# Lending dead SBUF as exp output buffers in a two-layer transformer kernel

## The chip, the cores and the metric

The kernel runs on one core of one Trainium2 chip. The metric is device time in microseconds (us) of one execution. The kernel before ran at a median of 1637.42 us in three runs.

## The reference, cut to what matters

Two identical layers are applied to a sequence of 2048 positions of width 512. Each is attention with 32 heads of 16 columns, then a feed-forward block with 1792 hidden columns. Both layers use the same weights.

```python
# inside _A_ref, which sees the layer-normed x
scores = jnp.einsum("bhqd,bhkd->bhqk", q, k) * (Dh ** -0.5)
p = _softmax(scores, axis=-1)
o = jnp.einsum("bhqk,bhkd->bhqd", p, v)
# the whole network
x = x + _A_ref(_layernorm(x, axis=-1), A_wqkv, A_wo)
x = x + _B_ref(_layernorm(x, axis=-1), B_w1, B_b1, B_w2, B_b2)
x = x + _A_ref(_layernorm(x, axis=-1), A_wqkv, A_wo)
x = x + _B_ref(_layernorm(x, axis=-1), B_w1, B_b1, B_w2, B_b2)
```

## The kernel before

The work is cut into 4096 score tiles of 128 keys by 512 query columns. For each tile TensorE (PE) makes the scores in PSUM, some engine makes the exponentials, and PE multiplies them with V (the "PV matmuls"). ScalarE (ACT) makes most exponentials with its own exp, two or three tiles in one instruction, into a ring of 15 SBUF units of 128x512 called PT. VectorE (DVE) makes the others by integer arithmetic on the bits, into other buffers; such a tile costs PE four PV matmuls in place of one. A unit of PT is free again when its PV matmul has read it.

The Python file is a planner: it runs a list scheduler with a cost model, and writes one fixed instruction order for each engine with semaphore waits. So a change of buffers changes the order of everything behind it. The PV matmuls go pass by pass (a pass is one group of heads for one segment of queries) through one PSUM bank. A pass must end, and VectorE must copy or add its result, before the PV matmuls of the next pass can begin.

The parts that matter, with cuts marked `# ...`:

```python
PT_RING = 15
PTLOW = 5
PTURG = 6
# ...
    def units(self, n):            # n free units at equal distances
        free = sorted(self.s.pools["pt"])
        # ...
    def exps(self):
        # ...
            if self.units(n) is None:              # no buffer: ScalarE waits
                self.starved = n
                yield ("cond", lambda n=n: self.units(n) is not None)
        # ...
            dst = T["PT"][:, run[0]:run[-1] + 1:step, :]
            yield _Op("act", 0.065 + 0.4267 * n, lambda e, src=src, dst=dst: e.activation(
                out=dst, in_=src, func=ACT.Exp, scale=0.25), # ...
    def pvs(self):
        # ...
            def urge():            # priority of the PV matmuls; small goes first
                return 0.5 if len(pools["pt"]) < PTURG or len(pools["du"]) < DUURG else PVP
        # ... whose tile is read first, ScalarE's (aq) or VectorE's (dq)
                        order = [self.aq[k], self.dq[k]]
                        if len(pools["pt"]) > PTLOW:
                            order.reverse()
```

Two marks count free units: with fewer than 6 free the PV matmuls become urgent, and with more than 5 free PE reads VectorE's tiles before ScalarE's. Where PE would idle, the planner puts filler matmuls that are meant to keep its clock up (with more of them the mean granted clock was 0.989 in e9 against 0.985, and in e10 0.987 against 0.987 in the same call); the constant `WARM` (0.38) says how busy it wants PE to be.

The softmax here doesn't subtract the row's maximum and nothing guards it: scores larger than these inputs give would overflow.

## Time and profile before

| | kernel before |
|---|---|
| span of the profiled run | 1631.0 us |
| ScalarE busy / idle | 1565.6 / 65.5 us |
| tiles on ScalarE / VectorE | 3254 / 842 |
| ScalarE waits on PV matmuls (no free unit) | 17.4 us |
| ScalarE waits for scores | 10.7 us |

The first line of the page (busy time of each engine, share of the span, instructions), and the first line of the chain that ended last:

```profile
PE 1443.1 (88%) x13642; PEld 417.7 (26%) x13794; DVE 1336.9 (82%) x2579; ACT 1565.6 (96%) x1413; POOL 111.9 (7%) x143
...
ACT 70%; PE 26%; DVE 2%; issue 1%; DMA 0%; POOL 0%
```

The groups with shapes kept apart. The columns are line, engine, operation, output<-input, shapes, count, then busy us and mean ns of one, then the idle time of the engine before them and what ended it:

```profile
L1313 ACT ACTIVATE pt<-ps 128x1024 bf16<-128x1024 f32 x815 | 848.6, 1100 | 15.1 <-PE ps L1374 9.3 <-PE ps L1059 4.9
L1313 ACT ACTIVATE pt<-ps 128x1536 bf16<-128x1536 f32 x541 | 821.8, 1519 | 15.9 <-PE ps L1374 8.0 <-PE ps L1059 5.7
...
L1204 DVE TENSOR_SCALAR du<-ps 128x512 uint16<-128x512 f32 x631 | 427.2, 685 | 132.9 <-PE ps L1059 126.5
...
L1204 DVE TENSOR_SCALAR dh<-ps 128x512 uint16<-128x512 f32 x113 | 77.5, 686 | 19.7 <-PE ps L1059 18.6
...
L1204 DVE TENSOR_SCALAR kt<-ps 128x512 uint16<-128x512 f32 x98 | 67.2, 686 | 22.2 <-PE ps L1059 21.3
```

The waits of ScalarE (who waited for whom: us in total, times, longest us):

```profile
ACT pt L1313 <- PE ps L1374: 17.4, 12, 3.5
ACT kt L645 <- PE ps L635: 14.9, 2, 13.7
ACT pt L1313 <- PE ps L1059: 10.7, 27, 1.4
```

ScalarE is the bound: it is busy for 96% of the span. L1313 is the exp, L1374 the PV matmul, L1059 the score matmul, L1204 the first step of VectorE's exp; its three counts add up to 842 tiles. Only the first line of the waits is about exp buffers; the second is the start, where the first projection is awaited. The exp line is busy 1487.1 us for 3254 tiles (the page's group of both shapes), 0.457 us per tile on average.

### The profile page before, as it was taken

The page shows a single profiled execution, that of the slowest core. Times are in us where ns is not written, and L with a number is a line of the kernel's source. Part 1 is how long each engine was busy: PE and PEld are TensorE (multiplying, and loading weights), DVE is VectorE, ACT ScalarE, POOL GpSimd, SP SyncE. Part 2 cuts the span into 40 slices and gives each one's busy share as a digit, 9 for nine tenths or more (in the row PEclk, how much of TensorE's full clock was granted, in tenths as well). Part 3 has the DMA queues.
Part 4 walks back from the last instruction along what each step waited for, and adds up shares of the span by engine and source line. Part 5 has one row for each costly group of instructions (what it writes and reads, how often), then busy time and mean ns, then how long its engine had stood idle before and what let it go on. Part 6 is the DMA issues. An engine that isn't in the chain of part 4 may idle for free.

```text
span 1631.0 us, 32568 instructions
## 1 busy us (share of the span) xinstructions
PE 1443.1 (88%) x13642; PEld 417.7 (26%) x13794; DVE 1336.9 (82%) x2579; ACT 1565.6 (96%) x1413; POOL 111.9 (7%) x143
## 2 busy tenths in 40 slices
PE   6998888898988989899898998888989889889997
PEld 2222222222222222222222222222222222233334
DVE  6579889778887797887888878998988997898883
ACT  5999999999999999999999999988999999999995
POOL 3200000000000000000100001010000000000000
PEclk9999999999999999999999999998999999999999
DMA  5100001100111001110111001001101100011121
GB/s 172 23 1 1 1 14 27 33 1 20 42 31 33 1 21 40 34 33 1 24 42 33 27 1 27 27 2 33 40 8 33 33 14 11 5 34 40 31 63 39
DMA packets 88317, 44.82 MB, mean 27 GB/s; under 512 B 33645, under 2 KB 88174, under 8 KB 88174
## 3 DMA queue, kind: packets, MB, share of 16 engines
q1 hardware_dynamic: 88174, 42.75, 9.8%
q8 instruction: 110, 1.80, 0.5%
q14 instruction: 33, 0.27, 0.1%
HBM read 33.03 MB, written 2.10 MB: 22 GB/s over the span
## 4 chain that ended last, share of the span: by engine, by line
ACT 70%; PE 26%; DVE 2%; issue 1%; DMA 0%; POOL 0%
ACT pt L1313 66%; PE ps L1374 8%; PE ps L1059 8%; ACT g L850 3%; PE ps L635 3%; PE ps L817 2%; PE ps L863 2%; PE ps L632 1%; PE ps L744 1%; ACT L850 1%; PE ps L1046 1%; ACT L1313 1%; DVE du L1204 0%; DVE du L1267 0%; DMA x<-in_A_x_dram 0%
## 5 line engine op out<-in xcount | busy, mean ns | idle before, releaser
L1313 ACT ACTIVATE pt<-ps 128x1536 bf16<-128x1536 f32 (+1 forms) x1357 | 1487.1, 1267 | 31.0 <-PE ps L1374 17.4
L1059 PE MATMUL ps<-qp,kt 32*128 32x512 bf16 x4096 | 550.3, 387 | 140.0 <-ACT pt L1313 111.1
L1204 DVE TENSOR_SCALAR du<-ps 128x512 uint16<-128x512 f32 x631 | 427.2, 685 | 132.9 <-PE ps L1059 126.5
L1374 PE MATMUL ps<-pt,v 128*17 128x512 bf16 (+1 forms) x3656 | 450.5, 361 | 2.9 <-DVE kt L707 0.8
L1374 PE MATMUL ps<-du,vc 128*17 128x512 bf16 (+1 forms) x2115 | 328.8, 360 | 0.8 <-DVE du L1267 0.7
L1059 PEld LDWEIGHTS ps<-qp,kt 32*128 32x128 bf16 x4096 | 143.8, 91 | 697.2 <-ACT pt L1313 334.6
L1267 DVE TENSOR_SCALAR du<-du 128x2048 uint16<-128x2048 uint16 (+1 forms) x319 | 218.2, 688 | 2.8
L1374 PE MATMUL ps<-du,v 128*17 128x512 bf16 (+1 forms) x705 | 170.6, 360 | 0.8 <-DVE kt L1267 0.5
L1023 POOL TENSOR_SCALAR qp<-q,mask 128x512 bf16<-128x512 bf16 (+1 forms) x92 | 68.6, 745 | 1285.2 <-PE ps L1059 1276.0
L1374 PEld LDWEIGHTS ps<-pt,v 128*17 128x17 bf16 x3656 | 103.8, 88 | 149.7 <-issue 118.2
L1265 DVE TENSOR_SCALAR du<-du 128x1024 uint16<-128x1024 uint16 (+1 forms) x319 | 129.9, 414 | 3.3
L863 PE MATMUL ps<-w,g 128*128 128x512 bf16 x396 | 115.7, 385 | 10.7 <-issue 5.4
L817 PE MATMUL ps<-xf,wr 128*128 128x512 bf16 (+1 forms) x420 | 113.4, 362 | 8.0 <-issue 5.6
L1374 PE MATMUL ps<-dh,vc 128*17 128x512 bf16 (+1 forms) x375 | 110.2, 365 | 0.0
L1374 PEld LDWEIGHTS ps<-du,vc 128*17 128x17 bf16 x2115 | 87.5, 90 | 62.1 <-issue 33.8
L1204 DVE TENSOR_SCALAR dh<-ps 128x512 uint16<-128x512 f32 x113 | 77.5, 686 | 19.7 <-PE ps L1059 18.6
L831 DVE TENSOR_SCALAR g<-ps,hb1t 128x512 bf16<-128x512 f32 (+1 forms) x112 | 79.7, 712 | 16.1 <-PE ps L817 15.3
L1204 DVE TENSOR_SCALAR kt<-ps 128x512 uint16<-128x512 f32 x98 | 67.2, 686 | 22.2 <-PE ps L1059 21.3
L1046 PE MATMUL ps<-w 128*32 128x512 bf16 x713 | 70.2, 397 | 0.1
L1374 PE MATMUL ps<-kt,vc 128*17 128x512 bf16 (+1 forms) x366 | 67.1, 340 | 0.0
L1374 PEld LDWEIGHTS ps<-du,v 128*17 128x17 bf16 x705 | 43.8, 89 | 27.7 <-issue 16.4
L1267 DVE TENSOR_SCALAR dh<-dh 128x1024 uint16<-128x1024 uint16 x113 | 47.7, 422 | 1.0
(74 smaller groups left out, 959.9 us busy)
## 6 DMA issues: line engine op xcount, KB each, us to landing
wr<-in_B_w_dram SPq DMA_DIRECT2D x59, 256.0 KB, 2.9
wr<-in_A_wqkv_dram SPq DMA_DIRECT2D x24, 256.0 KB, 2.8
wr<-in_A_wo_dram SPq DMA_DIRECT2D x18, 256.0 KB, 2.8
x<-in_A_x_dram SPq DMA_DIRECT2D x4, 512.0 KB, 8.4
out_dram<-x SPq DMA_DIRECT2D x16, 128.0 KB, 1.7
w<-in_B_w_dram SPq DMA_DIRECT2D x1, 1792.0 KB, 11.1
g<-in_A_wqkv_dram SPq DMA_DIRECT2D x3, 512.0 KB, 6.2
kt<-in_B_w_dram SPq DMA_DIRECT2D x4, 256.0 KB, 3.2
```

The lines of the kernel that those rows point to most:

```text
L817: fns = [lambda e, dc=dc, j=j, pb=pb: e.matmul(pb, lhsT=T["WR"][w][:, 256 * dc + 128 * j:256 * dc + 128 * j + 128], rhs=T["XF"][:, dc, q], ...
L831: yield _Op("dve", 0.21 + n / 966, lambda e, fc=fc, pb=pb: e.tensor_scalar(T["G"][:, fc, q], pb, T["HB1T"][:, fc:fc + 1], None, op0=ALU.ad ...
L850: fns.append(lambda e, g=g: e.activation(out=g, in_=g, func=ACT.Gelu_apprx_tanh))
L863: fns = [lambda e, fc=fc: e.matmul(pb, lhsT=T["G"][:, fc, q], rhs=T["W2"][:, fc, :], start=(fc == 0), stop=False) for fc in range(NFC)]
L1023: yield _Op("pool", 0.1 + 0.6 * w / 512, lambda e, s=s, q=q, i=i, t=t, w=w: e.tensor_scalar(T["QP"][:, s, w * i:w * i + w], q, T["MASK"][: ...
L1046: fns.append(lambda e, o=o, a=a, m=m: e.matmul(o, lhsT=T["W2"][:, 0, m * a:m * a + m], rhs=T["W2"][:, 1, :], start=True, stop=True, tile_p ...
L1059: return (lambda e: e.matmul(o, lhsT=lhsT, rhs=rhs, start=True, stop=True, tile_position=(32 * a, 0)), ["K%d.%d.%d" % (l, gb, kt // 4), "Q ...
L1204: yield _Op("dve", 0.68, lambda e: e.tensor_scalar(u, self.bank(b), E_SCALE, E_BIAS, op0=ALU.mult, op1=ALU.add), reads=["B.%d" % b], write ...
L1265: yield _Op("dve", 0.08 + 0.14 * n, lambda e: e.tensor_scalar(U[:, 1, 0:n, :], U[:, 0, 0:n, :], SHIFT, None, op0=ALU.add), reads=key[0], w ...
L1267: yield _Op("dve", 0.08 + 0.28 * n, lambda e: e.tensor_scalar(U[:, 2:4, 0:n, :], U[:, 0:2, 0:n, :], 2 * SHIFT, None, op0=ALU.add), reads=k ...
L1313: yield _Op("act", 0.065 + 0.4267 * n, lambda e, src=src, dst=dst: e.activation(out=dst, in_=src, func=ACT.Exp, scale=0.25), reads=["B.%d" ...
L1374: op.fns.append(lambda e, o=o, lhsT=q[0][0][m], rhs=q[0][1][:, n * m:n * m + n], a=a, st=st, sp=sp: e.matmul(o, lhsT=lhsT, rhs=rhs, start= ...
```

## The change

Two places in SBUF are dead for a time: columns of K of layer two until that layer's K is written (chunks 3 and 2, four units each), and 16 KB of each partition of V of layer one, sixteen units, once the partial sums kept there are merged. The change lends them to ScalarE's exps as further blocks of units. The trace of before shows when: K chunk 2 from 85 to 782 us, K chunk 3 from 111 to 978 us, V from 1094 us to the end. So there are 23 units in most of layer one, 19 for a while, 15 around the layer boundary, and 31 afterwards. The core of the diff:

```diff
+LEND = (3, 2)
-        T["PT"] = sb([128, PT_RING, 512], BF16, "pt")
+        pt = sb([128, PT_RING, 512], BF16, "pt")
+        T["PT"] = [pt[:, :, :]] + [T["K"][1][:, :, 512 * c:512 * c + 512] for c in LEND]
+        T["PT"].append(vf[0][:, 0:8192].rearrange("p (n q) -> p n q", q=512))
# ...
+                if c in LEND:                      # before K of layer two is written
+                    yield ("need", ("k1", c))
# ...
     def units(self, n):
-        free = sorted(self.s.pools["pt"])
+        for lo, hi in self.blocks:                 # a run lies in one block
+            free = sorted(u for u in self.s.pools["pt"] if lo <= u < hi and u not in self.closed)
# ...
+    def lend_units(self):
+        for i, c in enumerate(LEND):
+            self.s.spawn(self.lent(c, *self.blocks[1 + i]), 4)
+        for gb in range(4):
+            yield ("need", ("otn", NL - 1, self.segs[NL - 1][0], gb))
+        for u in range(*self.blocks[-1]):
+            yield ("rel", "pt", u)
+
+    def lent(self, c, lo, hi):
+        for kind in "KVQ":
+            for i in range(4):
+                yield ("need", (kind, 0, 4 * c + i if kind == "V" else i, c))
+        for u in range(lo, hi):
+            yield ("rel", "pt", u)
+        for t in range(4 * c, 4 * c + 4):
+            yield ("need", ("xready", t, 2))
+        self.closed.update(range(lo, hi))
+        for u in range(lo, hi):
+            yield ("take", ("pt", u))
+        yield ("give", ("k1", c))
```

The planner's marks (5 and 6 free units) were left as they were.

More of the change, by code (lines that the diff above doesn't have):

```diff
@@ L1283, in units @@
     def units(self, n):
-        free = sorted(self.s.pools["pt"])
-        for i in range(len(free) - n + 1):
-            if n == 1:
+        for lo, hi in self.blocks:
+            free = sorted(u for u in self.s.pools["pt"] if lo <= u < hi and u not in self.closed)
+            if free and n == 1:
                 return free[:1]
-            for j in range(i + 1, len(free)):
-                run = [free[i] + (free[j] - free[i]) * k for k in range(n)]
-                if all(r in free for r in run):
-                    return run
@@ L1292, in units, with unit @@
-        return None
+            for i in range(len(free) - n + 1):
+                for j in range(i + 1, len(free)):
+                    run = [free[i] + (free[j] - free[i]) * k for k in range(n)]
+                    if all(r in free for r in run):
+                        return run
+        return None
+    def unit(self, run):
+        b = [lo <= run[0] < hi for lo, hi in self.blocks].index(True)
+        lo = self.blocks[b][0]
+        step = run[1] - run[0] if len(run) > 1 else 1
+        return self.T["PT"][b][:, run[0] - lo:run[-1] - lo + 1:step, :]
@@ new lines, in setup_units @@
+    def setup_units(self):
+        self.blocks, self.alias, self.closed = [(0, PT_RING)], {}, set()
+        for c in LEND:
+            lo = self.blocks[-1][1]
+            self.blocks.append((lo, lo + NDC))
+            for i in range(NDC):
+                self.alias[lo + i] = ["K1.%d.%d" % (i, c)] + ["XL.%d" % t for t in range(4 * c, 4 * c + 4)]
+        lo = self.blocks[-1][1]
+        self.blocks.append((lo, lo + 16))
+        for i in range(16):
+            self.alias[lo + i] = ["PART.1.%d" % (i // 2)]
@@ new lines, in pkeys @@
+    def pkeys(self, u):
+        return ["PT.%d" % u] + self.alias.get(u, [])
+    def lend_units(self):
[17 more added lines that the diff above has]
+        yield ("give", ("k1", c))
@@ L1309, in exps @@
                 yield ("take", ("pt", r))
-            step = run[1] - run[0] if n > 1 else 1
             src = self.bank(SLOTS[sl][0], n).rearrange("p (j q) -> p j q", j=n)
-            dst = T["PT"][:, run[0]:run[-1] + 1:step, :]
+            dst = self.unit(run)
             yield _Op("act", 0.065 + 0.4267 * n, lambda e, src=src, dst=dst: e.activation(
                 out=dst, in_=src, func=ACT.Exp, scale=0.25),
-                reads=["B.%d" % b for b in SLOTS[sl][:n]], writes=["PT.%d" % r for r in run])
+                reads=["B.%d" % b for b in SLOTS[sl][:n]], writes=[k for r in run for k in self.pkeys(r)])
             for r, (pi, kt, a) in zip(run, cells):
@@ L1318, in exps @@
                 gb, ts = self.heads(seg, g)
-                self.aq[(pi, a)].append(([T["V"][l][:, kt, 8 * gb + 2 * a + t, 0:17] for t in ts], T["PT"][:, r, :],
-                                         ["V%d.%d" % (l, kt), "V%d1" % l, "PT.%d" % r], ("pt", r), True, kt))
+                self.aq[(pi, a)].append(([T["V"][l][:, kt, 8 * gb + 2 * a + t, 0:17] for t in ts], self.unit([r])[:, 0, :],
+                                         ["V%d.%d" % (l, kt), "V%d1" % l] + self.pkeys(r), ("pt", r), True, kt))
             yield from self.slot_done(sl)
@@ L1414, in run @@
         s.pool("pt", range(PT_RING))
+        self.setup_units()
         s.pool("qp", range(QP_RING))
@@ L1429, in run @@
         s.spawn(self.morebuf(), 4)
+        s.spawn(self.lend_units(), 4)
         s.spawn(self.solo(), 4)
```

## The prediction

> **What bounds the kernel now.** ScalarE. The page's first part gives ACT 1565.6 us of the 1631.0 us span (96%), PE 88%, VectorE (DVE) 82%. The chain of waits puts 70% on ACT, 66% on the exp line alone. The groups show 815 exps of 128x1024 (mean 1100 ns) and 541 of 128x1536 (1519 ns): ACT does 3254 of the 4096 score tiles at about 0.51 us each, DVE the other 842. [...] More buffers cannot shorten an exp.
>
> **What the change can remove.** The idle time of ACT before exps that ends at a PV matmul, a wait for a free output buffer: 17.4 us in 12 waits (groups and waits views). ACT's other idle time (start 17 us, waits for scores 10.7 us, end about 13 us) has nothing to do with buffers. By windows of the waits view, against each loan's opening and closing (timeline of the evacuations):
> - K of layer two, chunk 2: free from its last Q copy (85 us) to its last residual add (782 us); chunk 3: 111 to 978 us. Waits inside: 2.1 us at 96, 1.5 us at 110.
> - V of layer one: free from 1094 us, when the eighth partial sum is merged and transposed. Waits after it: 2.05 us at 1104, 3.5 us at 1113, 0.8 us at 1484.
> - 1001 to 1096 us, where neither is lent: 7.4 us. These stay. They belong to short passes that merge partial sums through the single PV bank.
>
> So about 10 us of 17.4 us can go, all of it on the critical path, as ACT has no slack there.
>
> **What it adds.** No instruction, no bytes. Exps write and PE reads other SBUF addresses; [...] I expect unchanged exp durations. No trace yet shows it. The copy of K for chunks 2 and 3 must now wait until lent units are drained; they are closed at the residual add, some 20 us before that copy, so no wait.
>
> **What it moves.** The planner is a list scheduler. Its rules compare the number of free units with 5 and 6; with 23 or 31 units the PV matmuls of ACT's tiles become urgent only at a backlog of 18 or 26 instead of 10. Rebuilding the ring's filling from the trace (exp tiles begun minus PV weight loads), the mean backlog is 6 to 7 of 15, and 10 or more about 10% of the time. It should grow where units are lent; VectorE's tiles go first, freeing its buffers slightly earlier. Where ACT no longer stalls, DVE has less chance to take tiles: each tile fewer on DVE costs ACT 0.5 us. I expect DVE's count within 842 plus or minus 25, either sign, about 12 us. The tail grows by at most 1 us of deferred PV.
>
> **Prediction.** About 10 us removed, a few given back: 1630 us, range 1613 to 1642. Faster by over 2% 0.04, within 2% 0.94, slower by over 2% 0.02.
>
> **What would show it.** ACT waits on PV matmuls fall from 17.4 to about 7 us, those left lying at 1000 to 1096 us; none over 0.5 us at 85 to 980 us or after 1100 us. Exp means by form unchanged within 1%. DVE first-step count 817 to 867.
>
> **What would make it wrong.** The changed order lets DVE take many more tiles (70 more would give over 2%), or fewer; deferred PV pushes an output projection late and starves the layer boundary or the tail; the K copy waits for lent units; writes to those places cost more.

## The result, and the profile after

The changed kernel ran at a median of 1631.7 us (1629.38 to 1634.02, 4 runs) against 1636.1 us (1634.48 to 1638.18, 4 runs). The ratio is 0.9972 with a 95% interval of 0.9953 to 0.9992. Ratios are the mean time of one kernel's runs over that of the other's of the same rounds, so not quite the ratio of the medians. It is a small but real gain, within 2% and close to the forecast of 1630.

The same lines for the changed kernel. The exp is now L1360, PV L1421, scores L1064, VectorE's first step L1209.

```profile
PE 1430.3 (88%) x13701; PEld 418.1 (26%) x13838; DVE 1355.2 (83%) x2612; ACT 1560.7 (96%) x1402; POOL 111.6 (7%) x143
...
ACT 58%; PE 36%; DVE 3%; issue 1%; DMA 1%; POOL 0%; ACTq 0%
```

```profile
L1360 ACT ACTIVATE pt<-ps 128x1024 bf16<-128x1024 f32 x761 | 792.7, 1084 | 6.8 <-PE ps L1064 5.8 <-PE ps L1421 0.2
L1360 ACT ACTIVATE pt<-ps 128x1536 bf16<-128x1536 f32 x455 | 687.8, 1512 | 23.4 <-PE ps L1421 13.0 <-PE ps L1064 8.6
...
L1209 DVE TENSOR_SCALAR du<-ps 128x512 uint16<-128x512 f32 x650 | 440.1, 685 | 112.7 <-PE ps L1064 106.2
...
L1360 ACT ACTIVATE v<-ps 128x1536 bf16<-128x1536 f32 x54 | 80.4, 1489 | 3.1 <-PE ps L1421 2.0 <-PE ps L1064 0.2
L1209 DVE TENSOR_SCALAR dh<-ps 128x512 uint16<-128x512 f32 x111 | 76.2, 686 | 12.1 <-PE ps L1064 9.2 <-PE ps L870 0.4
...
L1209 DVE TENSOR_SCALAR kt<-ps 128x512 uint16<-128x512 f32 x98 | 67.3, 686 | 15.8 <-PE ps L1064 14.6
...
L1360 ACT ACTIVATE kt<-ps 128x1536 bf16<-128x1536 f32 x37 | 56.1, 1515 | 0.6 <-PE ps L1064 0.3
```

```profile
ACT kt L648 <- PE ps L638: 14.7, 2, 13.4
ACT pt L1360 <- PE ps L1064: 14.4, 36, 1.3
ACT pt L1360 <- PE ps L1421: 13.2, 11, 4.1
...
ACT v L1360 <- PE ps L1421: 2.0, 5, 0.7
...
ACT kt L1360 <- PE ps L1064: 0.3, 1, 0.3
ACT v L1360 <- PE ps L1064: 0.2, 1, 0.2
```

What these lines say:

- The lent places cost nothing. An exp of three tiles takes 1489 ns into V and 1515 ns into K, against 1512 ns into the ring. PE's PV matmuls of 512 columns take 382 ns from V's units and 386 ns from the ring's.
- The waits for units hardly fell: 13.2 + 2.0 = 15.2 us, from 17.4. Nearly all of them (13.0 + 2.0) now stand before exps of three tiles, 8.0 of 17.4 before.
- VectorE makes 650 + 111 + 98 = 859 tiles, 17 more. ScalarE is busy 4.9 us less, about as much as the 4.4 us between the medians. That is 0.29 us for each tile moved, less than the 0.457 above. Part of the rest may be overlap that was lost: two exps in a row overlap in time, by about 170 ns in the kernel before (1357 exps last 815 x 1100 + 541 x 1519 ns and one of 745 ns, 1719 us in sum, and cover 1487.1 us), and in the trace 54 exps begin after a wait, 39 before. This was not tested.
- The waits for scores grew from 10.7 to 14.9 us (14.4 + 0.3 + 0.2), and in the chain ScalarE's share fell from 70% to 58% while PE's grew from 26% to 36%.

By place, read off the gaps before single exps in the two traces, the waits for units moved like this (sums of the gaps; one wait of 0.2 us at 50 us is left out in both):

| window, us | lent | before | after |
|---|---|---|---|
| 86 to 1001 | K (until 978) | 3.6 | 9.2 |
| 1001 to 1097 | nothing (V from 1094) | 7.2 | 3.5 |
| from 1097 | V | 6.3 | 2.2 |

So V's loan removed waits, but in K's window new ones came, the longest at a place where the kernel before had none. In the timeline the columns are start, duration, engine and work, and in brackets the idle time before it:

```profile
853.89 1.17 ACT L1360 ACTIVATE pt<-ps 128x1024 bf16<-128x1024 f32 x1
859.12 1.45 ACT L1360 ACTIVATE pt<-ps 128x1536 bf16<-128x1536 f32 x1 [4.06 <-PE ps L1421]
```

```profile
857.71 0.69 DVE L707 COPY v<-ps 128x512 f32<-128x512 f32 x1 [1.91 <-PE ps L1421]
```

The copy on VectorE empties the PV bank at the end of a pass. ScalarE got its unit only after the PV matmuls of the next pass could begin. Just before, PE was not full of useful work: 13 of its 22 matmuls from 853.6 to 857.0 were fillers. Part of this wait goes with the clock: e9 and e11 below have the same exp in the same place of the order (number 723, counted from 0), no half-clock stretch before it, and waits of 2.72 and 2.52 us. With such a stretch just before it waits about 4.06 us in the changed kernel, e1 and e3 alike. In e9:

```profile
855.57 6.89 ACT L1360 ACTIVATE pt<-ps 128x1536 bf16<-128x1536 f32 x6 [2.72 <-PE ps L1421]
```

How full were the units? Rebuilt from each trace (exp tiles begun minus PV weight loads of ScalarE's tiles, sampled as each exp begins), the mean number in use went from 6.7 to 9.9 between 120 and 780 us, and from 6.6 to 12.5 between 1130 and 1600 us, with at most 25 of the 31 in use. The planner used more of what it was given; its marks, which count free units, allow that, and e4 tests them.

The pool was not always full when ScalarE waited. By the same count 18 of 19 units were in use when the 4.06 us wait began, but 16 of 23 at the 1.84 us wait at 337 us, 12 of 19 at the 1.07 us wait at 881 us, and 8 to 15 of 31 at the waits after 1097 us. The planner fixes beforehand which units an exp writes, so it can wait for these while others are free. Its three units must also lie in one block at equal distances, and nearly all waits that are left stand before exps of three tiles. Whether this rule causes some of them no run tested.

### The profile page after: what moved, and what is told of

Same layout as the page of the kernel before. It is cut to its first block, busy times and chain, and to the rows that moved or that the text cites. A ratio compares the mean times of both kernels' runs of the same rounds, so it can differ in the third digit from the quotient of the medians.

```text
span 1629.9 us, 32720 instructions
## 1 busy us (share of the span) xinstructions
PE 1430.3 (88%) x13701; PEld 418.1 (26%) x13838; DVE 1355.2 (83%) x2612; ACT 1560.7 (96%) x1402; POOL 111.6 (7%) x143
## 4 chain that ended last, share of the span: by engine, by line
ACT 58%; PE 36%; DVE 3%; issue 1%; DMA 1%; POOL 0%; ACTq 0%
ACT pt L1360 49%; PE ps L1064 11%; PE ps L1421 11%; PE ps L868 4%; ACT v L1360 4%; PE ps L822 4%; PE ps L638 3%; ACT g L855 3%; ACT kt L1360 2%; PE ps L635 1%; DVE du L1209 1%; PE ps L749 1%; PE ps L1051 1%; ACT L855 1%; DMA xf<-xln 1%
## 5 line engine op out<-in xcount | busy, mean ns | idle before, releaser
L1360 ACT ACTIVATE pt<-ps 128x1024 bf16<-128x1024 f32 (+1 forms) x1217 | 1335.7, 1244 | 30.2 <-PE ps L1064 14.4
L1064 PE MATMUL ps<-qp,kt 32*128 32x512 bf16 x4096 | 545.5, 387 | 149.6 <-ACT pt L1360 109.5
L1209 DVE TENSOR_SCALAR du<-ps 128x512 uint16<-128x512 f32 x650 | 440.1, 685 | 112.7 <-PE ps L1064 106.2
L1421 PE MATMUL ps<-pt,v 128*17 128x512 bf16 (+1 forms) x3205 | 450.9, 364 | 2.3 <-ACT pt L1360 1.0
L1064 PEld LDWEIGHTS ps<-qp,kt 32*128 32x128 bf16 x4096 | 141.9, 91 | 700.6 <-ACT pt L1360 304.1
L1421 PE MATMUL ps<-du,vc 128*17 128x512 bf16 (+1 forms) x2178 | 305.1, 360 | 1.6 <-DVE du L1272 1.1
L1421 PE MATMUL ps<-du,v 128*17 128x512 bf16 (+1 forms) x726 | 140.3, 363 | 2.4 <-DVE du L1272 0.9
L1421 PEld LDWEIGHTS ps<-pt,v 128*17 128x17 bf16 x3205 | 107.6, 88 | 125.8 <-issue 96.7
L1270 DVE TENSOR_SCALAR du<-du 128x1024 uint16<-128x1024 uint16 (+1 forms) x329 | 136.6, 424 | 2.6
L1360 ACT ACTIVATE v<-ps 128x1536 bf16<-128x1536 f32 (+1 forms) x77 | 102.6, 1354 | 4.0 <-PE ps L1421 2.0
L1421 PE MATMUL ps<-dh,vc 128*17 128x512 bf16 (+1 forms) x369 | 105.5, 360 | 0.1
L1421 PEld LDWEIGHTS ps<-du,vc 128*17 128x17 bf16 x2178 | 83.0, 89 | 58.5 <-issue 26.5
L836 DVE TENSOR_SCALAR g<-ps,hb1t 128x512 bf16<-128x512 f32 (+1 forms) x112 | 79.9, 713 | 16.8 <-PE ps L822 15.1
L1209 DVE TENSOR_SCALAR dh<-ps 128x512 uint16<-128x512 f32 x111 | 76.2, 686 | 12.1 <-PE ps L1064 9.2
L1209 DVE TENSOR_SCALAR kt<-ps 128x512 uint16<-128x512 f32 x98 | 67.3, 686 | 15.8 <-PE ps L1064 14.6
L1360 ACT ACTIVATE kt<-ps 128x1536 bf16<-128x1536 f32 (+1 forms) x52 | 71.6, 1382 | 0.7 <-PE ps L1064 0.3
L1421 PE MATMUL ps<-kt,v 128*17 128x512 bf16 (+1 forms) x264 | 63.1, 365 | 0.1
```

The costliest lines, as they stand in the source:

```text
L836: yield _Op("dve", 0.21 + n / 966, lambda e, fc=fc, pb=pb: e.tensor_scalar(T["G"][:, fc, q], pb, T["HB1T"][:, fc:fc + 1], None, op0=ALU.ad ...
L1064: return (lambda e: e.matmul(o, lhsT=lhsT, rhs=rhs, start=True, stop=True, tile_position=(32 * a, 0)), ["K%d.%d.%d" % (l, gb, kt // 4), "Q ...
L1209: yield _Op("dve", 0.68, lambda e: e.tensor_scalar(u, self.bank(b), E_SCALE, E_BIAS, op0=ALU.mult, op1=ALU.add), reads=["B.%d" % b], write ...
L1270: yield _Op("dve", 0.08 + 0.14 * n, lambda e: e.tensor_scalar(U[:, 1, 0:n, :], U[:, 0, 0:n, :], SHIFT, None, op0=ALU.add), reads=key[0], w ...
L1421: op.fns.append(lambda e, o=o, lhsT=q[0][0][m], rhs=q[0][1][:, n * m:n * m + n], a=a, st=st, sp=sp: e.matmul(o, lhsT=lhsT, rhs=rhs, start= ...
```

## The experiments

Two theories stood at first. **W (waits)**, the prediction's: the gain is the waits that the loans take away. **S (share)**: the gain is tiles that move to VectorE, and the waits only move elsewhere. A third, **C (clock)**, came up after the first runs. All kernels gave correct results. "PV waits" and "score waits" below are the sums of the lines of ScalarE's waits view in each run's one profiled execution. "Clock" is the mean granted TensorE clock over the timed runs (for the kernel before, over those of the same call as e1).

| run | median us | ratio to before | 95% interval | VectorE tiles | ScalarE busy | PV waits | score waits | clock |
|---|---|---|---|---|---|---|---|---|
| before | 1636.1 | 1 | | 842 | 1565.6 | 17.4 | 10.7 | 0.988 |
| changed | 1631.7 | 0.9972 | 0.9953 to 0.9992 | 859 | 1560.7 | 15.2 | 14.9 | 0.985 |
| e1 K loan only | 1640.4 | 1.0024 | 1.0009 to 1.0039 | 854 | 1561.5 | 20.4 | 19.7 | 0.981 |
| e2 V loan only | 1643.06 | 1.0045 | 1.0027 to 1.0063 | 851 | 1564.9 | 13.4 | 18.5 | 0.983 |
| e3 share capped | 1642.71 | 1.0046 | 1.0032 to 1.0061 | 844 | 1568.4 | 15.7 | 20.7 | 0.982 |
| e4 urgency by use | 1629.35 | 0.9960 | 0.9946 to 0.9975 | 844 | 1565.1 | 11.0 | 15.1 | 0.991 |
| e5 ring of 11 | 1686.25 | 1.0298 | 1.0270 to 1.0326 | 848 | 1567.7 | 54.8 | 23.9 | 0.989 |
| e6 ring of 11, loans | 1639.11 | 1.0023 | 0.9969 to 1.0076 | 858 | 1565.2 | 17.6 | 17.6 | 0.984 |
| e7 SWAP 0.55 | 1656.33 | 1.0117 | 1.0080 to 1.0154 | 846 | 1566.2 | 24.0 | 27.7 | 0.985 |
| e8 SWAP 0.55, loans | 1629.42 | 0.9949 | 0.9917 to 0.9981 | 865 | 1559.8 | 11.1 | 20.7 | 0.984 |
| e9 fillers, loans | 1630.27 | 0.9964 | 0.9939 to 0.9990 | 859 | 1560.1 | 13.8 | 16.3 | 0.989 |
| e10 fillers | 1639.84 | 1.0019 | 0.9993 to 1.0044 | 842 | 1566.8 | 17.3 | 19.7 | 0.987 |
| e11 fillers, capped | 1640.24 | 1.0025 | 1.0003 to 1.0048 | 844 | 1567.3 | 14.3 | 17.3 | 0.987 |
| e12 marks set anew | 1613.81 | 0.9864 | 0.9841 to 0.9886 | 868 | 1555.1 | 7.1 | 13.0 | 0.995 |

One caution on the ledger: the profiled run of the kernel before was one of its fastest (1632.95 us, clock 0.992). e10 has the same order of real work, and its profile shows the same busy time and PV waits (1566.8 and 17.3 us) but 19.7 us of score waits. So in these two profiles busy time and PV waits repeat to within 1.2 us, and score waits do not.

### e1 and e2: one loan at a time

```diff
 # e1: V's units are never released
-        for u in range(*self.blocks[-1]):
-            yield ("rel", "pt", u)
 # e2: K's units are never released
-            self.s.spawn(self.lent(c, *self.blocks[1 + i]), 4)
+            yield ("give", ("k1", c))
```

> Only the eight buffers in K of layer two are lent, those in V of layer one are not. Theory W (the gain is waits for output buffers that go away): the K loan is worth the 3.6 us of waits that lie in its window in the kernel before, so about 1632.5 us against 1636.1, with the waits after 1094 us back as they were (about 6 us). Theory S (the gain is tiles that move from ScalarE to VectorE, while the waits only move elsewhere): this build gives VectorE 854 tiles (842 before, 859 with both loans), so 12 x about 0.43 us = 5 us less ScalarE work, about 1631 us, with ScalarE's waits on PV matmuls in total not under 15 us.

> Only the sixteen buffers in V of layer one are lent, those in K are not. W: 6.4 us of waits lie after 1094 us in the kernel before, so about 1630 us, with the waits before 1094 us as they were (11 us). S: this build gives VectorE 851 tiles, 9 more than before, so about 4 us less ScalarE work, about 1632 us; nothing new before 1094 us, as the schedule is the same up to there. The two theories differ little in time here; the places of the waits tell more.

Both came out slower than the kernel before, by 0.2% and 0.4%, which neither theory had expected. e1 has the 12 more VectorE tiles and the 4.1 us less ScalarE work that S expected, and PV waits of 20.4 us, also as S said. What eats that up is 9.0 us more score waits than in the profile of before. e2's PV waits fell to 13.4 us, and score waits took that back too. The gaps say where K's loan acts: e1 has the changed kernel's 9.2 us of PV waits in K's window, wait for wait, and e2 has 4.1 us there. So the two loans together gain, each alone loses, and the remainder lies in waits for scores. That led to C.

The clock qualifies this. Take the line of time against clock of the kernel before (fitted under e9) and compare each run with it at the run's own clock. By this estimate e1 is 3.0 us faster than the kernel before, e2 2.2 us slower, the changed kernel 6.7 us faster, e3 1.5 us slower and e4 3.8 us faster. So e1 loses only together with its low clock (0.981 against 0.988). Whether that clock caused the loss or came from the same schedule is not shown.

### e3: both loans, VectorE's share held down

```diff
+CAP, CAP0 = 0.204, 10
     def next_d(self, used, start, pop=True):
         tok = self.s.tokens
+        if self.nd > CAP * self.scored + CAP0:
+            return None
```

> Both loans as in the changed kernel, but VectorE may take a tile only while its tiles are at most 0.204 of all scored tiles plus 10: 844 tiles in this build, 842 in the kernel before, 859 in the changed one. W: the loans still take the waits away, so the time stays at 1631 to 1632 us. S: the gain is the tiles, so it goes: 1635 to 1639 us.

W fails: with both loans and 15 tiles fewer than the changed kernel the time is 1642.71 us, and no gain is left. S is right that the gain goes; the kernel even falls 0.46% behind the one before, more than S's 1635 to 1639. The page's first line:

```profile
PE 1441.9 (88%) x13810; PEld 420.2 (26%) x13944; DVE 1345.2 (82%) x2607; ACT 1568.4 (95%) x1405; POOL 110.5 (7%) x143
```

ScalarE is busy 7.7 us more than in the changed kernel (1568.4 against 1560.7), with PV waits hardly changed (15.7 and 15.2 us). The spans of the two profiles differ by 13.3 us; besides the 7.7 us of busy time, 5.8 us are score waits (20.7 against 14.9). The cap acted late: up to 1100 us VectorE began 574 tiles in both kernels, and after that 270 in place of 285. So the new waits in K's window are all still there (9.2 us). The cap also changes the order of the work behind it, and e7 shows that a new order alone can cost over 1%, so the time of this one run does not prove S.

### e4: marks that count units in use

```diff
# ... open_units counts the units of the ring and of the blocks lent at the time
+    def busy(self):
+        return self.open_units - len(self.s.pools["pt"])
-                return 0.5 if len(pools["pt"]) < PTURG or len(pools["du"]) < DUURG else PVP
+                return 0.5 if self.busy() > PT_RING - PTURG or len(pools["du"]) < DUURG else PVP
-                        if len(pools["pt"]) > PTLOW:
+                        if self.busy() < PT_RING - PTLOW:
```

> Both loans, but the planner's two rules compare the number of units in use with the old marks (urgent from 10 in use, ScalarE's tiles first from 10 in use) in place of the number of free units with 6 and 5, so lent units are a true reserve and not filled as a matter of course. W: ScalarE's waits on PV matmuls inside the loans' windows fall to under 2 us in total, the 7 us at 1000 to 1096 us stay, time 1630 us or less. S: the waits fall by several us, but this build gives VectorE only 844 tiles, so the time is 1633 to 1636 us, no better than the changed kernel.

```profile
ACT pt L1366 <- PE ps L1064: 14.2, 32, 0.8
ACT pt L1366 <- PE ps L1427: 10.4, 9, 2.9
...
ACT v L1366 <- PE ps L1427: 0.6, 1, 0.6
```

This is the counterpart to e3, and here S's time fails. With 844 tiles, two more than the kernel before, and the same ScalarE busy time (1565.1 us), it gains 0.4%: the PV waits fell by 6.4 us to 11.0. W's time holds, though not its "under 2 us" inside the windows: 3.2 us remain in K's and 3.3 us after 1096 us. The mean number of units in use was back at 6.5 between 120 and 780 us. So here a reserve that is not filled goes with fewer waits, and one that is filled brings tiles. Both are worth about the same here. The changed kernel took the second way.

Between 120 and 780 us VectorE began 368 tiles in the kernel before, 385 in the changed one and 368 in e4. In this window e1 has 385 too and e2 367. So VectorE's extra tiles there come with K's loan and with the backlog. Which of the two marks brings them was not separated.

### e5 and e6: a smaller ring

```diff
-PT_RING = 15
+PT_RING = 11
```

> The kernel before with 11 buffers in the ring in place of 15, no loan. If buffers are what ScalarE lacks when there are few of them, its waits on PV matmuls grow from 17 us to 60 or more and the time to 1675 to 1700 us. If buffers do not matter at all, under 1% slower.

> The changed kernel (both loans) with 11 buffers in its own ring. If lent buffers are as good as the ring's own, most of the loss of the 11-buffer ring comes back: 1635 to 1650 us, waits on PV matmuls about 20 us, those left lying before 86 us and at 1000 to 1096 us, where nothing is lent. If lent places are worse (slower writes, waits of the K copy), it stays above 1660 us.

```profile
ACT pt L1313 <- PE ps L1374: 54.8, 53, 4.1
```

Four units fewer cost 3.0%, and the PV waits grew to 54.8 us, slightly less than expected. With the loans the same ring is level with the kernel before (1.0023, an interval that holds 1), and PV waits are 17.6 us. The waits lie elsewhere than expected: 8.2 us in K's window and 5.1 us after 1097 us, where units are lent, and 3.6 us from 1001 to 1097. So the loans make up for four lost units. Since they bring 8 or 16, this does not show that a lent unit is worth as much as one of the ring. The gain in the case under study was small probably because 15 units were enough most of the time.

### e7 and e8: a nudge to the schedule

```diff
-SWAP = 0.5
+SWAP = 0.55
```

> The kernel before with one planner constant, SWAP, at 0.55 in place of 0.5; it lets ScalarE trade a tile to VectorE slightly later. It stands for the scatter of the schedule: a harmless edit that reorders everything behind it. If the kernel before was tuned onto a lucky schedule, this one is 10 to 25 us slower (1646 to 1660 us) and the loss is waits on PV matmuls (40 us in place of 17), with the tile count hardly changed (846). If the schedule is robust, within 4 us of 1636.

> The changed kernel with the same constant at 0.55. If the loans' true worth is that the schedule no longer depends on luck, this one stays at 1627 to 1633 us (865 tiles on VectorE) and the loans are worth 15 us or more in this pair, against 4 us in the pair under study. If the loans are worth a fixed 4 us, it is 4 us below its partner without loans.

The same edit costs the kernel before 1.17%, with 4 tiles more on VectorE, and costs the changed kernel nothing. In this pair the loans are worth 1.7% (0.9949 over 1.0117 is 0.983), against 0.28% in the pair under study. Only part of e7's loss is PV waits (24.0 us, not the 40 expected); the score waits grew as well. This is one nudge and no statistics, but it says that the size of the gain depends on how well the other kernel's constants happened to fit. It is also a warning for all single edits here, e3 and e11 included: a reorder alone moved the kernel before by 20 us.

### e9, e10 and e11: more fillers, same order of work

Over 29 runs of the kernel before made beside these experiments, time follows the granted clock: from 1631.86 us at 0.990 to 1641.81 us at 0.981, a least-squares fall of 9.5 us per 0.01 (correlation -0.91). In the traces of the kernel before and the changed one the clock record is 1 or 0.5, never between, and up to the last five us the low stretches last 3.4 us (3 before, 9 changed), 6.8 us (1 and 2) or 10.2 us (1 and 0). The windows view shows, after a stretch at full clock for comparison, the one that goes with the 4.06 us wait (columns: window and its length, busy us of PE, weight loads, DVE, ACT and POOL, then the granted clock, DMA share and GB/s):

```profile
848.00:851.40 3.40, 2.67 (x24) 0.56 (x19) 2.73 (x7) 3.40 (x4) 0.27 (x1) 1.00 0.00 0
853.60:857.00 3.40, 3.40 (x22) 0.65 (x14) 2.20 (x6) 1.46 (x2) 0.00 (x0) 0.50 0.27 56
```

The five score matmuls within the second took 592 ns in the mean, against 387 over the whole run. The changed kernel's profile has 11 such stretches before the last five us, the one of before has 5; but that was one of its fastest runs, and e10, with the same order of real work and a clock of 0.984 in its profile, has 12. In the 6.8 us before each of the changed kernel's 11 drops the longest idle gap of PE was 1.53 us, and PE was busy 68% to 78% of that time. What makes the clock fall was not shown. C says that the low stretches eat part of the gain.

```diff
-WARM = 0.38
+WARM = 0.46
```

For all three pairs the order of real work on each engine stays the same; only fillers are added.

> The changed kernel with the planner's constant WARM at 0.46 in place of 0.38: the order of all real work on every engine is the same, only filler matmuls, which keep TensorE busy, are added (262 groups in place of 175). Theory C (part of the gain is lost because the changed schedule leaves TensorE more stretches at half clock): mean granted clock from 0.985 to 0.991 or more, ScalarE's waits for scores from 18 us to 14 us or less, time 1624 to 1628 us. If the clock is only a symptom, the time stays at 1630 to 1633 us; if fillers get in the way, it grows.

> The kernel before with WARM at 0.46, order of the real work unchanged (266 filler groups in place of 179). C: its clock is at 0.988 already, so the gain is smaller: clock 0.991 or more, 1630 to 1633 us. Together with the run of the changed kernel with the same constant this is the pair at nearly equal clock; theory S expects 5 to 8 us between the two.

> The capped kernel (both loans, 844 tiles on VectorE) with WARM at 0.46, order of the real work unchanged (313 filler groups in place of 218). It tells how much of the capped kernel's loss was share and how much clock. S at equal clock: as fast as the kernel before with the same constant, within 3 us, and 5 us or more behind the changed kernel with the same constant. If its loss was clock alone, it comes within 2 us of the changed kernel with the same constant.

C was not confirmed. In e9 the clock rose from 0.985 to 0.989, but the time of 1630.27 us is within the scatter of 1631.7, and score waits did not fall (16.3 us; the changed kernel has 14.9 by the view, not the 18 that the expectation names). In e10 neither clock (0.987, as the kernel before in the same call) nor time improved. So more fillers are no cure, and whether the low clock causes the score waits or goes with them stays open. The first lines of the pages of e9, e10 and e11:

```profile
PE 1466.5 (90%) x14183; PEld 425.8 (26%) x14183; DVE 1354.3 (83%) x2612; ACT 1560.1 (96%) x1402; POOL 112.0 (7%) x143
...
PE 1495.0 (91%) x14139; PEld 426.0 (26%) x14139; DVE 1336.9 (81%) x2579; ACT 1566.8 (95%) x1413; POOL 110.9 (7%) x143
...
PE 1473.9 (90%) x14321; PEld 426.6 (26%) x14321; DVE 1344.6 (82%) x2607; ACT 1567.3 (96%) x1405; POOL 110.7 (7%) x143
```

The three runs, made on one chip, speak for the share once more. With the same fillers, the loans are worth 0.55% (0.9964 over 1.0019 is 0.9945), and capping VectorE at 844 tiles takes all of it away (1.0025). S had expected 5 to 8 us between e9 and e10; it is 8.9 us by the means. At clocks of 0.989 and 0.987 the capped kernel is 10.0 us by the means behind the one with 859 tiles. Of the 8.9 us between their two profiled spans, 7.2 us are ScalarE's busy time (1567.3 against 1560.1). But e11 has e3's order of real work, so it is the same cap on the same schedule and no second one. Between the profiles of e9 and e10 (14.2 us) 6.7 us are busy time, 3.5 us PV waits and 3.4 us score waits, so with the same fillers the share is about half of the difference.

### e12: the marks set anew for the larger pool

```diff
-PTLOW = 5
-TOL = 0.2
-WARM = 0.38
-PTURG = 6
-DULOW = 1
+PTLOW = 8
+TOL = 0.25
+WARM = 0.46
+PTURG = 8
+DULOW = 2
```

> The changed kernel with the planner's marks set anew for the larger pool (PTLOW 8 and PTURG 8 free units in place of 5 and 6, DULOW 2 in place of 1, TOL 0.25 in place of 0.2) and WARM at 0.46. The marks make ScalarE's tiles be read earlier and leave free units as a reserve. This build gives VectorE 868 tiles. With fewer waits on PV matmuls (8 us or less) and about 4 us less ScalarE work than in the changed kernel, 1615 to 1622 us, which would beat both kernels.

```profile
PE 1466.1 (91%) x14158; PEld 426.1 (26%) x14158; DVE 1358.8 (84%) x2633; ACT 1555.1 (96%) x1405; POOL 109.9 (7%) x143
```

```profile
ACT pt L1360 <- PE ps L1064: 11.6, 34, 1.1
ACT pt L1360 <- PE ps L1421: 5.7, 6, 1.5
ACT v L1360 <- PE ps L1421: 1.4, 5, 0.4
```

At 1613.81 us it beats both kernels, 1.36% under the one before and better than expected. It has both currencies at once: 868 tiles on VectorE, 10.5 us less ScalarE work than before, and PV waits of 7.1 us. Whether these marks would also help the kernel without loans was not run, so the whole 1.36% is not the loans' alone. Nor is it the two marks' alone: TOL, DULOW and WARM changed with them, and only WARM was also tried by itself (e9). The set was picked from many that the planner's own cost model ranked; only this one was run.

## Why the prediction was right or wrong

- **The time** was right: 1630 forecast, 1631.7 measured, inside the range and within 2% as forecast.
- **ScalarE bounds the kernel, and no exp gets shorter**: right. The prediction's equal exps in other places were the author's expectation, which no trace yet showed; the changed kernel's trace agrees, 1489 and 1515 ns in lent places against 1512. The means of the ring's own two forms moved by 1.5% and 0.5%, so "within 1%" missed for one.
- **"So about 10 us of 17.4 us can go"**: this step failed. The PV waits fell by 2.2 us to 15.2. Where V is lent they did fall, from 6.3 to 2.2 us. Where K is lent they rose from 3.6 to 9.2 us, with single waits of 1.84 us at 337, 4.06 us at 859 and 1.07 us at 881, where the prediction expected none over 0.5 us. The 7.4 us (7.2 by the gaps) between 1001 and 1096 us, said to stay, fell to 3.5. The mistake was to read old waits as if the rest of the schedule stood still. The next paragraph of the prediction already named what undid it, the marks that count free units, but did not draw the conclusion: a pool that may be filled to the same margin can starve again. e4 supports it for K's window: with the marks on units in use, the PV waits there are 3.2 us in place of 9.2, and 11.0 us in all. It is not the whole account: in V's window the pool filled further too (12.5 in use in place of 6.6), and the waits fell all the same.
- **The backlog grows where units are lent**: right, from 6.7 to 9.9 and from 6.6 to 12.5 units in use.
- **VectorE's count within 842 plus or minus 25, either sign**: right, but treated as noise around the result. Its 17 tiles brought most of the result: 4.9 us less ScalarE work, and holding the count down takes the gain away (e3, e11, one schedule). A tile was worth 0.29 us, not the 0.5 of the prediction, whose 0.51 us per tile counts the time in which two exps overlap twice.
- **The copy of K does not wait for lent units**: right. In the waits view of the changed kernel the copies of K wait for their own projection matmuls alone (14.7 us on ScalarE, 10.8 us on VectorE).
- **The tail**: the last exp ended 29.0 us before the end in both profiles, at 1602.0 of 1631.0 and 1600.8 of 1629.9 us, within 0.1 us.
- **Not foreseen at all**: waits for scores, which take 10.7 us in the profile of the kernel before and 19.7 us in that of e10 with the same order of real work, and the granted clock, with which one kernel's time goes from 1631.86 us at 0.990 to 1641.81 us at 0.981.

So the total was right by luck: one term was overestimated (waits, 10 us forecast, 2.2 measured), while another, set at zero with a spread, came out at 4.9 us.

## What to carry to other kernels

Before adding buffers, look at every rule that counts free ones: if its marks stay, the new buffers can be filled and not kept as a reserve, and waits can come back elsewhere. Try new marks for the new pool in the same change (here 0.28% became 1.36%, with three other constants changed along, and not tried without the loans). When a list scheduler writes the order, account for a small gain as busy time plus each kind of wait, and try one harmless nudge on both kernels before believing a few tenths of a per cent.
